# A retention layer and a multiplicative feed-forward block on one core: key copies moved between engines, and one chunk's outputs put inside an output block

## The chip, the cores and the metric

The kernel runs on one core of a Trainium2 chip. The metric is the device time of one execution in microseconds (us); of several executions the median is taken. A core has TensorE (PE, matrix products, with its weight loads shown as PEld), VectorE (DVE), ScalarE (ACT) and GpSimd (POOL), and SyncE (SP), which here issues the transfers. Matrix products land in PSUM, which is divided into banks; GpSimd works on SBUF only in this kernel.

## What is computed

The reference has two parts. The first is a recurrence over 768 positions for 4 batches and 8 heads of 64 elements: a state decays by a head's own factor and takes in the outer product of key and value, and the query reads it. The second part takes the 3072 resulting rows of 512 through a feed-forward block whose hidden layer is the product of two projections.

```python
gamma = 1.0 - 2.0 ** (-5.0 - np.arange(H, dtype=np.float32))
for t in range(S):
    state = gamma[None, :, None, None] * state + np.einsum('bhd,bhe->bhde', k[:, :, t], v[:, :, t])
    y[:, :, t] = scale * np.einsum('bhd,bhde->bhe', q[:, :, t], state)
# ... y becomes x, 3072 rows of 512
a = x @ w1
b = x @ w2
h = a * b @ w3
return h @ w_out
```

## The kernel before

The recurrence is worked in chunks of 128 positions, 6 to a batch, 24 in all. For a chunk n the kernel casts keys to f16 (`k16`), transposes them on TensorE into a padded form `KP` in which the two heads of a pair lie in separate halves, forms the scores of keys against queries and masks them (`am`), scales the values (`VP`), and forms the outputs from `am`, `VP` and the state. The feed-forward work is cut into units, "a", "b" and "o" (512 columns of output for 128 rows). They wait in a queue, and each chunk's step pulls some of them between its own parts, so that TensorE has work while other engines prepare. Since `w3 @ w_out` has no nonlinearity before it, it is multiplied once at the start (`W3O`).

The first four chunks are loaded two to a tile (a pair), with even and odd positions interleaved. Each half of a chunk's keys therefore either stays on its 64 partitions or is moved to the other 64 ("moved"):

```python
def pair_casts(n, moved, names="kv", eng=None):
    m, c = divmod(n, 2)
    rows = slice(c * 64, c * 64 + 64)
    t = 1 - c if moved else c
    to = slice(t * 64, t * 64 + 64)
    eng = eng or (nc.vector if moved else nc.gpsimd)
    # ... k16s[n] is allotted
    if "k" in names:
        eng.tensor_copy(
            k16s[n][to, :].rearrange("i (h d) -> i h d", d=D),
            pair_in["k", m][rows, :].rearrange("i (h t d) -> i h t d", t=2, d=D)[:, :, t, :],
        )
    for r in range(2 if "v" in names else 0):
        eng.tensor_tensor(VP[n % 3][to, :, r, r * 64 : r * 64 + 64], ...)   # cut: values times decay

def transposes_back(n):
    kp, ps = KP[n % 2], kTs.pop(n)
    nc.scalar.copy(kp[0:64, :, 0, :], ps[0:64, :, :])
    cast_to(kp[64:128, :, 1, :], ps[64:128, :, :], False)     # False: ScalarE, True: VectorE
```

The part of the start in which chunks 2 and 3 are prepared, in program order. Each engine does its own share of it in this order:

```python
for n in (2, 3):
    pair_casts(n, False, "k")            # GpSimd
    pair_casts(n, True, "k")             # VectorE
by_rows(W1, ps, 2)                       # TensorE, first projection of block 0
q_back = q_transposes(1, True)
q_back(0)                                # VectorE: qT
q_back(1)
by_rows(W1, ps, 3, blocks=(0, 3))
transposes(2)                            # TensorE, then the two copies of transposes_back
by_rows(W1, ps, 3, blocks=(3, 8))
transposes_front(3, "psK")
# ...
nc.gpsimd.tensor_copy(W2[0][:, :], w2_st[0][:, :])
pair_casts(2, False, "v")                # GpSimd
pair_casts(3, False, "v")
cast_to(pa[0], ps[0], False)
cast_to(pa[1], ps[1], True)              # VectorE
cast_to(pa[2], ps[2], False)
scores(2, between=lambda: pair_casts(2, True, "v"))   # VectorE: am, two vp, am
cast_to(pa[3], ps[3], True)
transposes_back(3)
# ... casts of W2
by_rows(W2, ps, 0)
outputs(2, "psK")
scores(3)
```

The step of a later chunk, and an output unit:

```python
def step(n):
    # ...
    scores(n)
    fill.pull(share * 0.25, ready)
    t_new = kv(n)
    # ... casts, transfers of later chunks
    if n == 4:
        transposes(5)
    fill.pull(share * 0.25, ready)
    outputs(n)
    Tst[0] = t_new
    if n != 4:
        transposes(n + 1)
    fill.pull(share * 0.5, ready)

def o_unit(self, tb, between=None):
    psO = ps_f.tile([128, DM], FP, tag="psF", name="psO")
    for f in range(8):
        if f == 4 and between:
            between()
        nc.tensor.matmul(psO[:, :], lhsT=self.HT[:, f, tb * 128 : (tb + 1) * 128], rhs=W3O[f][:, :],
                         start=(f == 0), stop=(f == 7))
    # ... scaled copy by ScalarE and the transfer out
```

The last output unit is made in two column blocks, `for c0, c1 in ((0, 320), (320, 512))`.

Of the kernel before, what the change touches and what calls it, by code (L numbers as in the profile page):

```python
# [18 lines left out]
def kernel(  # L19
# [11 lines left out]
    nc = tc.nc  # L31
# [194 lines left out]
    def cast_to(dst, src, on_dve):  # L226
        if on_dve:
            nc.vector.tensor_copy(dst, src)
        else:
            nc.scalar.copy(dst, src)  # L230
# [11 lines left out]
    def bank(tag, shape, dtype, name):  # L242
        return (ps_t if tag == "psT" else ps_at).tile(shape, dtype, tag=tag, name=name)
# [59 lines left out]
# [7 lines that stand above are left out]
        if n not in k16s:  # L310
            k16s[n] = att.tile([128, 512], HP, tag="k16", name="k16", bufs=3)
        if "k" in names:
            eng.tensor_copy(
                k16s[n][to, :].rearrange("i (h d) -> i h d", d=D),
                pair_in["k", m][rows, :].rearrange("i (h t d) -> i h t d", t=2, d=D)[:, :, t, :],
            )
        for r in range(2 if "v" in names else 0):
            eng.tensor_tensor(  # L318
                VP[n % 3][to, :, r, r * 64 : r * 64 + 64],
                pair_in["v", m][rows, :].rearrange("j (p s t e) -> j p s t e", s=2, t=2, e=64)[:, :, r, t, :],  # L320
                VS2[rows, t, :].rearrange("j (p s) -> j p s", s=2)[:, :, r].unsqueeze(2).broadcast_to((64, NP, 64)),
                MULT,
            )
# [9 lines left out]
    def casts(n):  # L333
        if n >= NSTEP:
            return
        k32, v32 = chunk_in.pop(n)
        if n % 2 == 0:
            q_cast(n // 2)
        k16 = att.tile([128, 512], HP, tag="k16", name="k16", bufs=3)
        nc.gpsimd.tensor_copy(k16[:, :], k32[:, :])  # L340
        vp = VP[n % 3]

        for r in range(2):
            nc.gpsimd.tensor_tensor(  # L344
                vp[:, :, r, r * 64 : r * 64 + 64],
                v32[:, :].rearrange("j (p s e) -> j p s e", s=2, e=64)[:, :, r, :],
                VS[:, :].rearrange("j (p s) -> j p s", s=2)[:, :, r].unsqueeze(2).broadcast_to((128, NP, 64)),
                MULT,
            )
        k16s[n] = k16  # L350
# [30 lines left out]
    def by_dma(n):  # L381

        return n >= DT0 and n != DT0 + 1
# [16 lines left out]
    def queries(n, p):  # L400
        if n < DT0:
            return qTs[n][:, p, :]
        c = n % 2
        return qTd[n // 2][:, :, p, c * 64 : (c + 1) * 64]

    def transposes(n, tag="psT"):
        if n >= NSTEP:
            return
        if by_dma(n):
            kT, kp = kTs.pop(n), KP[n % 2]  # L410
            nc.scalar.copy(kp[0:64, :, 0, :], kT[0:64, :, :])  # L411
            nc.scalar.copy(kp[64:128, :, 1, :], kT[64:128, :, :])
            return
        transposes_front(n, tag)
        transposes_back(n)

    def transposes_front(n, tag):
        k16 = k16s[n]
        ps = bank(tag, [128, NP, 128], HP, "psT")
        for p in range(NP):  # L420
            nc.tensor.transpose(ps[:, p, :], k16[:, p * 128 : (p + 1) * 128], ident16[:, :])
        kTs[n] = ps

    def transposes_back(n):
        kp, ps = KP[n % 2], kTs.pop(n)
        nc.scalar.copy(kp[0:64, :, 0, :], ps[0:64, :, :])
        cast_to(kp[64:128, :, 1, :], ps[64:128, :, :], False)

    def scores(n, tags=("psA0", "psA1"), between=None):
        kp = KP[n % 2]  # L430
        am = att.tile([128, NP, 2, 128], HP, tag="am", name="am")
        for half in range(2):
            ps = bank(tags[half], [128, 2, 2, 128], FP, "psA")
            for i in range(2):
                p = half * 2 + i
                for r in range(2):
                    nc.tensor.matmul(  # L437
                        ps[:, i, r, :], lhsT=kp[:, p, r, :], rhs=queries(n, p), start=True, stop=True
                    )
            if half and between:  # L440
                between()
            nc.vector.tensor_tensor(  # L442
                am[:, half * 2 : half * 2 + 2, :, :].rearrange("j p s i -> j (p s) i"),
                ps[:, :, :, :].rearrange("j p s i -> j (p s) i"),
                (keep2 if n < 4 else keep)[:, :].unsqueeze(1).broadcast_to((128, 4, 128)),
                MULT,
            )
        ATs[n] = am

    def kv(n, tag="psK", eng=nc.gpsimd):  # L450
        k16, vp = k16s.pop(n), VP[n % 3]
        c = n % NCH
        if c == NCH - 1:
            return None
        ps = bank(tag, [128, NP, 128], FP, "psK")
        for p in range(NP):

            rhs = vp[:, p, :, :].rearrange("j s e -> j (s e)")
            rhs = bass.AP(rhs.tensor, rhs.offset, [list(rhs.ap[0]), [192, 2], [1, 64]])
            nc.tensor.matmul(  # L460
                ps[:, p, :], lhsT=k16[:, p * 128 : (p + 1) * 128], rhs=rhs, start=True, stop=True
            )
        t16 = att.tile([128, NP, 128], HP, tag="t16", name="t16")
        if c == 0:
            nc.vector.tensor_tensor(t16[:, :, :], ps[:, :, :], GS[:, :, :], MULT)
        else:
            s32 = att.tile([128, NP, 128], FP, tag="s32", name="s32")
            nc.vector.tensor_tensor(s32[:, :, :], ps[:, :, :], Tst[0][:, :, :], ADD)  # L468
            eng.tensor_tensor(t16[:, :, :], s32[:, :, :], GS[:, :, :], MULT)  # L469
        return t16  # L470

    def outputs(n, tag="psY"):
        am, vp = ATs.pop(n), VP[n % 3]
        c = n % NCH
        ps = bank(tag, [128, NP, 128], FP, "psY")
        for p in range(NP):
            nc.tensor.matmul(ps[:, p, :], lhsT=vp[:, p, 0, :], rhs=am[:, p, 0, :], start=True, stop=False)  # L477
            nc.tensor.matmul(ps[:, p, :], lhsT=vp[:, p, 1, :], rhs=am[:, p, 1, :], start=False, stop=(c == 0))  # L478
            if c > 0:
                nc.tensor.matmul(ps[:, p, :], lhsT=Tst[0][:, p, :], rhs=queries(n, p), start=False, stop=True)  # L480
        if n % 2 == 0:
            XT[n // 2] = xpool.tile([128, NP, 256], HP, tag="xt", name="xt")

        order = "p a (t i) -> p a t i"
        nc.vector.tensor_tensor(  # L485
            XT[n // 2][:, :, n % 2 * C : (n % 2 + 1) * C].rearrange("p a (i t) -> p a t i", t=2),
            ps[:, :, :].rearrange(order, t=2), YS[:, :, :].rearrange(order, t=2), MULT,
        )
# [107 lines left out]
    fill = Queue()  # L596
# [3 lines left out]
    def step(n):  # L600

        ready = n * C
        share = fill.available(ready) / (2 - n % 2)
        if n >= DT0 - 2:
            casts(n + 2)
# [3 lines that stand above are left out]
        if n < DT0 - 2:  # L609
            casts(n + 2)  # L610
        dma_transposes(n + 2)
        load_chunk(n + 4)
        if n % 2:
            q_transposes((n + 1) // 2)
        if n == 4:
            transposes(5)
        fill.pull(share * 0.25, ready)
        outputs(n)
        Tst[0] = t_new
        if n != 4:  # L620
            transposes(n + 1)
        fill.pull(share * 0.5, ready)

# [44 lines left out]
    cast_w3(7, w3_st[7])  # L668
    q_cast(0)
    pair_casts(0, False, "k")  # L670
    pair_casts(1, False, "k")
    pair_casts(0, False, "v")
# [28 lines left out]
    ffn = [Ffn(a, b - a) for a, b in zip(bounds, bounds[1:])]  # L701
# [5 lines left out]
    def four_banks(tags):  # L707
        got = []
        for t in tags:
            if t == "psF":  # L710
                got.append(ps_f.tile([128, 2, TB], FP, tag=t, name="psF"))
            else:
                got.append(bank(t, [128, 2, TB], FP, "psG"))
        return [t[:, :, :] for t in got]
# [10 lines left out]
    ps = four_banks(("psF", "psF", "psF", "psY"))  # L725
# [2 lines left out]
    by_rows(W1, ps, 1)  # L728
    for n in (2, 3):
        pair_casts(n, False, "k")  # L730
        pair_casts(n, True, "k")
    by_rows(W1, ps, 2)
    q_back = q_transposes(1, True)
    q_back(0)
# [18 lines left out]
    ps = four_banks(("psF", "psF", "psF", "psT"))  # L753
# [73 lines left out]
```

## Time and profile before

| | before |
|---|---|
| time, median of 3 | 196.28 us (195.66 to 196.31) |
| span of the profiled execution | 193.8 us |
| TensorE busy | 185.0 us (95%) |
| VectorE busy | 118.6 us (61%) |
| ScalarE busy | 98.8 us (51%) |
| GpSimd busy | 86.1 us (44%) |
| granted TensorE clock | 1.000 |

The lines of the profile name an engine, a line of the kernel, an operation, what it writes and reads (out<-in, by tile names), and shapes as partitions x elements and type; in square brackets stands the idle time of that engine just ahead, and what ended it. xN is the number of instructions merged into a row. Busy time of TensorE counts a matmul up to its modelled end, so consecutive ones overlap: how fast they follow each other is read from their starts. A wait that is put down to one engine may have been for another, when several had to be over.

### The profile page before, as it was taken

Reading aid. Unit: us, or ns where it says so; the run is one execution under the profiler, and the core shown is the slowest. Engines: PE = TensorE matmul, PEld = TensorE weight load, DVE = VectorE, ACT = ScalarE, POOL = GpSimd, SP = SyncE. Lnnn points to the kernel's source line nnn. Section 1 sums busy time; section 2 is a strip of 40 time slices with the busy share of each in tenths; the row PEclk is TensorE's granted clock in tenths of the full one; section 3 lists DMA queues with packets and bytes.
Section 4 is the critical chain, followed back from the end, with each engine's and each line's share of the span. In section 5 each row is a group of like instructions: output and inputs, shape, how many; then the busy total and the mean of one; then the engine's idle time right before and its main releaser. Section 6 shows DMA issues by size and latency. Waiting matters only on the chain.

```text
span 193.8 us, 4696 instructions
## 1 busy us (share of the span) xinstructions
PE 185.0 (95%) x1777; PEld 140.0 (72%) x1777; DVE 118.6 (61%) x221; ACT 98.8 (51%) x191; POOL 86.1 (44%) x146
## 2 busy tenths in 40 slices
PE   6798999879999999999999999999999999999993
PEld 2435658668796889778877787788778877887752
DVE  3226598799586768657565666575657665754220
ACT  6478565582454455355535554555455545533322
POOL 7600287828863738368152643852426432200000
PEclk9999999999999999999999999999999999999999
DMA  5999999999999999999999989969979931111004
GB/s 203 370 391 390 300 395 324 365 286 223 219 172 226 214 230 240 98 274 223 215 268 206 209 187 225 212 148 244 212 186 195 209 95 26 57 54 54 36 28 156
DMA packets 85030, 40.54 MB, mean 209 GB/s; under 512 B 61328, under 2 KB 80016, under 8 KB 85008
## 3 DMA queue, kind: packets, MB, share of 16 engines
q1 hardware_dynamic: 85008, 40.25, 89.5%
q8 instruction: 14, 0.23, 0.5%
q14 instruction: 8, 0.07, 0.2%
HBM read 29.36 MB, written 6.29 MB: 184 GB/s over the span
## 4 chain that ended last, share of the span: by engine, by line
PE 79%; DMA 10%; SPq 4%; ACT 2%; DVE 2%; POOL 1%; issue 1%; ACTq 0%; POOLq 0%
PE psF L508 39%; PE psO L534 20%; DMA stg<-in_moe_w_dram 5%; PE psA L437 5%; DMA q<-in_q_dram 4%; SPq L62 4%; PE psY L477 3%; PE psY L478 2%; PE psY L480 2%; PE psK L460 2%; DVE am L442 1%; PE psF L719 1%; PE psW L293 1%; PE psG L508 1%; PE psO L551 1%
## 5 line engine op out<-in xcount | busy, mean ns | idle before, releaser
L508 PE MATMUL psF<-xt,w 128*128 128x256 f16 (+1 forms) x736 | 85.0, 266 | 0.0
L508 PEld LDWEIGHTS <-w 128*128 128x128 f16 x768 | 68.2, 98 | 7.2
L524 DVE TENSOR_TENSOR ht<-pa,psF 128x256 f16<-128x256 f32 x88 | 36.5, 416 | 22.1 <-PE psF L508 12.9
L518 ACT COPY pa<-psF 128x256 f32<-128x256 f32 x84 | 31.2, 372 | 33.8 <-PE psF L508 33.4
L442 DVE TENSOR_TENSOR am<-psA,keep 128x512 f16<-128x512 f32 x48 | 31.0, 685 | 23.0 <-PE psA L437 22.8
L534 PE MATMUL psO<-w3o,ht 128*128 128x512 f16 x184 | 43.1, 379 | 0.0
L469 POOL TENSOR_TENSOR t<-s,GS 128x512 f16<-128x512 f32 x15 | 19.3, 1284 | 40.0 <-DVE s L468 40.0
L539 ACT ACTIVATE osb<-psO 128x512 f32<-128x512 f32 x23 | 13.7, 597 | 37.8 <-PE psO L534 37.8
L534 PEld LDWEIGHTS <-ht 128*128 128x128 f16 x184 | 17.9, 98 | 17.2 <-DVE ht L768 0.2
L344 POOL TENSOR_TENSOR vp<-v,VS 128x256 f16<-128x256 f32 x40 | 23.8, 616 | 5.5 <-DMA v<-in_v_dram 2.5
L327 POOL CAST q<-q 128x1024 f16<-128x1024 f32 x12 | 13.0, 1086 | 27.5 <-DMA q<-in_q_dram 27.5
L485 DVE TENSOR_TENSOR xt<-psY,YS 128x512 f16<-128x512 f32 x24 | 17.8, 742 | 3.6 <-PE psY L480 3.2
L477 PE MATMUL psY<-am,vp 128*128 128x128 f16 x96 | 16.8, 219 | 0.9 <-ACT kp L230 0.5
L478 PE MATMUL psY<-am,vp 128*128 128x128 f16 x96 | 16.7, 219 | 0.4 <-DVE vp L318 0.4
L437 PEld LDWEIGHTS <-kp 128*128 128x128 f16 x192 | 12.5, 98 | 5.3 <-ACT kp L230 0.9
L340 POOL CAST k<-k 128x512 f16<-128x512 f32 x20 | 12.2, 612 | 5.0 <-PE psK L460 3.4
L468 DVE TENSOR_TENSOR s<-psK,t 128x512 f32<-128x512 f32 x16 | 11.0, 688 | 3.0 <-PE psK L460 2.7
L251 DVE COPY w3t<-psW 128x1024 f16<-128x1024 f16 x8 | 5.5, 690 | 10.7 <-PE psW L259 8.4
L437 PE MATMUL psA<-qTd,kp 128*128 128x128 f16 x144 | 11.1, 219 | 0.0
L480 PE MATMUL psY<-qTd,t 128*128 128x128 f16 x60 | 10.8, 219 | 0.0
L411 ACT COPY kp<-kT 64x512 f16<-64x512 f16 x17 | 10.5, 618 | 0.4
L478 PEld LDWEIGHTS <-vp 128*128 128x128 f16 x96 | 9.4, 98 | 1.8 <-POOL vp L318 0.7
(80 smaller groups left out, 192.8 us busy)
## 6 DMA issues: line engine op xcount, KB each, us to landing
stg<-in_moe_w_dram SPq DMA_DIRECT2D x16, 512.0 KB, 7.8
q<-in_q_dram SPq DMA_DIRECT2D x12, 512.0 KB, 5.6
out_dram<-osb SPq DMA_DIRECT2D x23, 256.0 KB, 2.9
k<-in_k_dram SPq DMA_DIRECT2D x20, 256.0 KB, 5.4
v<-in_v_dram SPq DMA_DIRECT2D x20, 256.0 KB, 5.4
stg<-in_moe_w_out_dram SPq DMA_DIRECT2D x4, 512.0 KB, 8.0
stg<-in_k_dram SPq DMA_DIRECT2D x2, 512.0 KB, 10.5
stg<-in_v_dram SPq DMA_DIRECT2D x2, 512.0 KB, 8.0
```

Of the source, the lines that this page charges most:

```text
L344: nc.gpsimd.tensor_tensor(vp[:, :, r, r * 64 : r * 64 + 64], v32[:, :].rearrange("j (p s e) -> j p s e", s=2, e=64)[:, :, r, :], VS[:, :]. ...
L437: nc.tensor.matmul(ps[:, i, r, :], lhsT=kp[:, p, r, :], rhs=queries(n, p), start=True, stop=True)
L442: nc.vector.tensor_tensor(am[:, half * 2 : half * 2 + 2, :, :].rearrange("j p s i -> j (p s) i"), ps[:, :, :, :].rearrange("j p s i -> j ( ...
L469: eng.tensor_tensor(t16[:, :, :], s32[:, :, :], GS[:, :, :], MULT)
L477: nc.tensor.matmul(ps[:, p, :], lhsT=vp[:, p, 0, :], rhs=am[:, p, 0, :], start=True, stop=False)
L478: nc.tensor.matmul(ps[:, p, :], lhsT=vp[:, p, 1, :], rhs=am[:, p, 1, :], start=False, stop=(c == 0))
L480: nc.tensor.matmul(ps[:, p, :], lhsT=Tst[0][:, p, :], rhs=queries(n, p), start=False, stop=True)
L485: nc.vector.tensor_tensor(XT[n // 2][:, :, n % 2 * C : (n % 2 + 1) * C].rearrange("p a (i t) -> p a t i", t=2), ps[:, :, :].rearrange(orde ...
L508: nc.tensor.matmul(ps[:, i * w : (i + 1) * w], lhsT=W[d][:, (f + i) * 128 : (f + i + 1) * 128], rhs=XT[self.tok0 // TB][:, d, c0 : c0 + w] ...
L518: nc.scalar.copy(self.pa[f][:, :], ps[:, :])
L524: nc.vector.tensor_tensor(self.HT[:, f : f + TB // self.width, :].rearrange("p f n -> p (f n)"), self.pa.pop(f)[:, :], ps[:, :], MULT,)
L534: nc.tensor.matmul(psO[:, :], lhsT=self.HT[:, f, tb * 128 : (tb + 1) * 128], rhs=W3O[f][:, :], start=(f == 0), stop=(f == 7),)
```

## The change

The change has three parts in the program. The moved key casts of chunks 2 and 3 go from VectorE to ScalarE, to relieve VectorE at that point. The copy of the second half of chunk 2's padded keys goes from ScalarE to VectorE, so that the two halves are on two engines. In the step of chunk 5, the next queued output unit is taken out of the queue, and the chunk's outputs (with the padded-key copies of chunk 6) are issued between its fourth and fifth matmul; before, the outputs came first and the unit after. The amount of work is the same. The words that come with the change also speak of the last block as 320 + 192 columns; that is in the kernel before already, and the diff has no line for it.

```diff
@@ -310,7 +310,7 @@
         if "k" in names:
-            eng.tensor_copy(
+            (nc.scalar.copy if eng is nc.scalar else eng.tensor_copy)(
                 k16s[n][to, :].rearrange("i (h d) -> i h d", d=D),
                 pair_in["k", m][rows, :].rearrange("i (h t d) -> i h t d", t=2, d=D)[:, :, t, :],
             )
@@ -424,7 +424,7 @@
     def transposes_back(n):
         kp, ps = KP[n % 2], kTs.pop(n)
         nc.scalar.copy(kp[0:64, :, 0, :], ps[0:64, :, :])
-        cast_to(kp[64:128, :, 1, :], ps[64:128, :, :], False)
+        cast_to(kp[64:128, :, 1, :], ps[64:128, :, :], n == 2)
@@ -615,9 +615,14 @@
         fill.pull(share * 0.25, ready)
-        outputs(n)
+        if n == 5:
+
+            fill.units.pop(0)
+            ffn[1].o_unit(0, lambda: [outputs(n), transposes(6)])
+        else:
+            outputs(n)
         Tst[0] = t_new
-        if n != 4:
+        if n not in (4, 5):
             transposes(n + 1)
         fill.pull(share * 0.5, ready)
@@ -728,7 +733,7 @@
     for n in (2, 3):
         pair_casts(n, False, "k")
-        pair_casts(n, True, "k")
+        pair_casts(n, True, "k", nc.scalar)
```

## The prediction

> **What bounds the kernel now.** I read the page first, then the busy time by stretch, then the waits of TensorE alone, and last the timeline of the two places where TensorE waits. From the page:
>
> ```profile
> PE   6798999879999999999999999999999999999993
> PE 79%; DMA 10%; SPq 4%; ACT 2%; DVE 2%; POOL 1%; issue 1%; ACTq 0%; POOLq 0%
> ```
>
> The first line is TensorE's busy share in 40 slices of 4.85 us; after the eighth it is full to the last one. The second is the chain of work that ended last: 79% of it is TensorE. So time can be won only where TensorE waits. The busy time by stretch says where that is (columns: stretch and its length, then busy us of TensorE, weight loads, VectorE, ScalarE, GpSimd):
>
> ```profile
> 33.00:42.00 9.00, 7.33 (x81) 5.62 (x79) 7.18 (x13) 5.74 (x9) 6.46 (x8) 1.00 1.09 349
> 42.00:57.00 15.00, 15.00 (x206) 12.77 (x204) 12.00 (x23) 6.69 (x14) 10.64 (x14) 1.00 1.05 214
> 57.00:62.00 5.00, 4.79 (x60) 3.59 (x58) 3.44 (x7) 1.98 (x4) 2.33 (x4) 1.00 0.88 197
> 62.00:180.00 118.00, 118.00 (x1147) 94.92 (x1145) 74.97 (x144) 58.92 (x127) 51.53 (x68) 1.00 0.92 178
> ```
>
> From 33 to 42 us TensorE lacks 1.67 us, from 57 to 62 us 0.21 us, and from 62 to 180 us nothing. The change touches just the first and the third stretch. In the first, TensorE's own waits are:
>
> ```profile
> PE psY L477 <- ACT kp L230: 0.5, 1, 0.5
> PE psY L478 <- DVE vp L318: 0.4, 1, 0.4
> PE psA L437 <- ACT kp L230: 0.4, 1, 0.4
> PE psY L477 <- DVE am L442: 0.2, 1, 0.2
> ```
>
> They all belong to chunk 2. Its timeline (start, duration, engine, line, out<-in):
>
> ```profile
> 34.45 1.17 DVE L313 CAST k<-stg 64x512 f16<-64x512 f32 x2 [1.10 <-DMA stg<-in_k_dram]
> 34.48 1.62 POOL L313 CAST k<-stg 64x512 f16<-64x512 f32 x2 [0.24 <-DMA stg<-in_k_dram]
> 35.39 0.40 PE L421 MATMUL psT<-ident,k 128*128 128x128 f16 x4
> ...
> 35.54 0.74 DVE L228 COPY qT<-psTq 128x512 f16<-128x512 f16 x2
> ...
> 35.88 0.58 ACT L426 COPY kp<-psT 64x512 f16<-64x512 f16 x1 [3.70 <-PE psT L421]
> ...
> 36.20 0.67 DVE L228 COPY stg<-psF 128x512 f32<-128x512 f32 x1
> 36.48 0.58 ACT L230 COPY kp<-psT 64x512 f16<-64x512 f16 x1
> ...
> 37.50 0.69 DVE L442 TENSOR_TENSOR am<-psA,keep 128x512 f16<-128x512 f32 x1 [0.62 <-PE psA L437]
> 37.52 2.70 POOL L318 TENSOR_TENSOR vp<-stg,VS 64x256 f16<-64x256 f32 x4 [0.33 <-PE psA L437]
> ...
> 38.22 1.52 DVE L318 TENSOR_TENSOR vp<-stg,VS 64x256 f16<-64x256 f32 x2
> ```
>
> The reader should follow one string through these lines: keys land, k is cast, PE transposes it, ScalarE copies one half of kp (35.88) and only then the other (36.48, done 37.06), scores, am, and then VectorE scales the values (vp), which ends at 39.74. The second am ends at 40.46, and the last outputs of chunk 2 start at 40.52. The first wait in the list above, put down to kp, is really one for VectorE's vp: kp was done at 37.06, the first of the two vp at about 38.98. In the other stretch:
>
> ```profile
> 58.00 1.29 DVE L442 TENSOR_TENSOR am<-psA,keep 128x512 f16<-128x512 f32 x2
> 58.03 0.61 PE L508 MATMUL psF<-xt,w 128*128 128x128 f16 x8
> ...
> 58.75 0.22 PE L477 MATMUL psY<-am,vp 128*128 128x128 f16 x1
> ...
> 59.35 0.22 PE L477 MATMUL psY<-am,vp 128*128 128x128 f16 x1
> ...
> 59.68 1.89 PE L534 MATMUL psO<-w3o,ht 128*128 128x512 f16 x8
> ```
>
> Chunk 5's outputs stand right behind its scores and one b unit. They start only when the first am is done, and their second half only when the second am is (58.00 + 1.29 = 59.29). No wait view lists this, because the tail of the matmul before covers the gap; it shows in the start times.
>
> **What the Trainium skill says.** (1) "TensorE: Matmul & The Clock Gate", section "Back-to-back issue gap": an isolated warm matmul takes N/2.4 + 2.5 ns, 56 ns for 128 columns and 216 ns for 512. The trace agrees: starts are 0.055 us apart at 128 columns (58.75, 58.80, 58.86), and the eight 512-column ones take 59.68 to 61.40, 0.215 each. I use these steps below. (2) "GPSIMD Engine Reference", section "1. Specifications": GpSimd shares its SBUF interfaces with VectorE and suffers when VectorE runs in a two-port mode. The trace agrees: VectorE's key cast of this form took 420 ns before GpSimd had begun and 719 ns beside it; GpSimd's own took from 607 ns (the shortest of four) to 860 ns. (3) "VectorE: DVE Perf Modes", section "Why PSUM operands drop a tier": from PSUM VectorE keeps at most the packed 2x mode, so an f16 copy stays quick there. The trace: 406 to 408 ns for a 128x512 f16 copy of q from PSUM, against 578 to 580 ns for ScalarE's copies of the same length. (4) "PSUM — Partial Sum Buffer", section "PSUM bank collisions raise a hardware error": two engines may use one bank at once only in different groups of 32 partitions. The halves of kp are partitions 0 to 63 and 64 to 127, so the hardware lets both copies run at once; but no engine pair in the trace before reads one bank together, so it does not show whether this program's generated waits let them.
>
> **The change, part by part.**
>
> *Moved casts to ScalarE.* Removed from VectorE: two casts, 1.17 us from 34.45. Added to ScalarE, idle for 3.70 us until 35.88: two copies of 512 elements; its copies of that length take 0.58, so 34.45 to 35.03 and to 35.62 (an estimate; no f32 SBUF copy of that size is in the trace). GpSimd, now alone, should need about 0.61 each: 34.48 to 35.09 to 35.70 instead of 36.10. Chunk 2's transposes can start at about 35.17 instead of 35.39, behind the three matmuls before them. psT is ready at about 35.60 and ScalarE's half of kp runs 35.66 to 36.24, 0.22 earlier. VectorE can copy qT from about 34.97 (psTq was complete near 34.92), to 35.78.
>
> *Second half of kp to VectorE.* If both run together: 35.78 to 36.19 at 0.41 each, beside ScalarE's. Scores then have both halves at 36.24 and start at 36.28 instead of waiting to 37.12. VectorE casts pa from 36.19 to 36.86 and does the first am at about 36.87 to 37.56, 0.63 earlier than 37.50 to 38.19. Earlier than this hardly helps: the values of chunks 2 and 3 were issued at 30.83 us and took 6.6 us in the view of DMA issues, so vp cannot start before 37.43 (GpSimd's did at 37.52). vp: 37.58 to 39.10; second am to 39.82; last outputs 0.64 earlier. I allow 0.6 to 0.7 us.
>
> From there on TensorE runs without a gap and VectorE too, up to 48 us, and both start earlier by the same amount. What could stop the shift is a landing. The view of DMA issues gives 43.03 + 5.3 = 48.3 for chunk 5's values (used by GpSimd at 51.0) and 46.91 + 5.8 = 52.7 for chunk 6's (used at 53.7). The latter leaves 1.0 us, enough for 0.65. The last w2 tile is cast by 42.57 and used at 44.16. I let the shift pass whole.
>
> *Outputs of chunk 5 inside an output block.* No instruction is added. Four 512-column matmuls (4 x 0.216 = 0.86 us) now stand between the b unit and the outputs. Without waits the outputs would have started at 58.03 + 8 x 0.055 = 58.47 and ended at 58.47 + 12 x 0.055 = 59.13; the block began at 59.68, so 0.55 us is lost now. After: block's first half 58.47 to 59.33; outputs from 59.33, second half from 59.66, after am's 59.29. Both waits vanish: 0.55 us. xt would be ready about 60.9 and is used after chunk 6's scores at 61.3. It fits.
>
> *320 + 192.* The last block is cut that way already in the kernel before; the diff does not touch it. Zero.
>
> Sum with the copies together: 0.65 + 0.55 = 1.2 us, 196.28 - 1.2 = 195.1 us.
>
> **The rivals.** *The two kp copies are put in order* (one PSUM bank, two engines, ScalarE's first). Then VectorE waits to 36.26, copies to 36.67, casts pa to 37.34, and the first am runs 37.36 to 38.05: only 0.14 earlier, as VectorE itself is what am waits for. With 0.55 that is 0.7 us, 195.6. For it: a bank is the unit that a cautious generator would guard; against it: the halves lie on different partitions. I give it 45%. *The values' transfer takes the place of the wait*: vp starts at 37.43 at the earliest, so part one can't yield more than 38.22 - 37.43 = 0.8 us. This caps the gain at 1.35 us, 194.9. *ScalarE becomes the bound*: its casts reach to 35.62, psT is ready at 35.60, so it costs some 0.05 us; if a cast took the 1.05 us of the page's 1024-element casts, kp would be 0.8 us later, chunk 2 would lose about 0.6 us and the total would be 196.3. The 0.585 us of a 512-element f32 copy from PSUM speaks against it (10%). *The shift is swallowed by later loads*: GpSimd waits for q, k and v from 62.24 on, but chunk 8's casts end near 66 and its scores come several us later; nothing in TensorE's row shows it (10%).
>
> **Range and chances.** Weighing 195.1 (half), 195.6 (most of the rest) and the small chances of no gain gives 195.3; I take 195.2. The runs of before spread from 195.66 to 196.31, so the time itself is uncertain by some 0.3. Range 194.5 to 195.9. A change of 2% is 3.9 us, more than all of TensorE's idle time in both stretches (1.67 + 0.21), so faster by that is 0.01, slower 0.02, within 0.97.
>
> **What would show it.** Right: VectorE's kp copy near 36 us overlapping ScalarE's; scores at about 36.3; last outputs of chunk 2 near 39.9; four 512-column matmuls ahead of chunk 5's outputs and no uneven start times in them; TensorE full in 57 to 62. Wrong: kp on VectorE after 36.25 (the ordered rival); vp still at 38.1 or later; a TensorE wait after 42 us; a ScalarE cast much longer than 0.6 us; or a new TensorE gap around the output block.

## The result, and the profile after

| | before | changed |
|---|---|---|
| time, median | 196.21 us (195.66 to 196.31, 4 runs) | 195.09 us (195.02 to 195.39, 4 runs) |
| ratio to before | | 0.9952, 95% interval 0.993 to 0.9973 |
| span of the profiled execution | 193.8 us | 193.0 us |
| start of chunk 2's key casts (the landing of its keys) | 34.45 us | 34.44 us |
| from there to the last two output pairs of chunk 2 | 6.07 us | 5.58 us |
| from chunk 5's scores to the unit behind chunk 6's scores | 4.27 us | 4.00 us |
| from the key casts to the end of the span | 159.36 us | 158.59 us |

The changed kernel is 0.5% faster. By the interval that is 0.53 to 1.37 us (0.27% and 0.70% of 196.21). The last four rows are read from start times in the timelines; the end of the span is taken from the trace in full (193.81 and 193.04 us), while the recorded expectations go by the page's figure, rounded to 0.1. The rows are counted from the key casts because the keys' landing differs from execution to execution (34.44 to 35.26 us in the profiles of this study), and everything behind it moves along.

First TensorE's busy share in 40 slices and the chain that ended last, from the page of the changed kernel:

```profile
PE   6789999789999999999999999999999999999993
PE 70%; DMA 17%; POOL 4%; DVE 3%; SPq 2%; issue 1%; ACT 1%; POOLq 0%; DVEq 0%; ACTq 0%
```

TensorE is full as before, but its share of the chain fell from 79% to 70% and transfers rose from 10% to 17%: just before 60 us the chain now reaches back from TensorE, through ScalarE's copies, into the transposing transfer of chunk 6's keys and the load of its values. The busy time by stretch (same columns as before):

```profile
33.00:42.00 9.00, 7.18 (x84) 5.79 (x82) 6.37 (x12) 6.40 (x10) 5.72 (x8) 1.00 1.10 351
42.00:57.00 15.00, 15.00 (x209) 12.78 (x206) 12.00 (x22) 6.67 (x14) 11.29 (x14) 1.00 1.01 210
57.00:62.00 5.00, 4.91 (x58) 3.66 (x56) 3.72 (x8) 2.49 (x5) 1.83 (x4) 1.00 0.96 194
```

Between 33 and 42 us TensorE is busy for less than before (7.18 against 7.33 us), although it starts 84 matmuls there instead of 81. Busy time doesn't show the gain, starts do: the last two output pairs of chunk 2 began at 40.52 us before and begin at 40.02 now. TensorE's waits in that stretch, and chunk 2's timeline:

```profile
PE psY L478 <- DVE vp L318: 0.6, 1, 0.6
PE psT L421 <- POOL k L313: 0.4, 1, 0.4
PE psY L477 <- ACT kp L230: 0.4, 1, 0.4
PE psA L437 <- DVE kp L228: 0.2, 1, 0.2
PE psY L477 <- DVE am L442: 0.2, 1, 0.2
```

```profile
34.44 1.26 ACT L313 CAST k<-stg 64x512 f16<-64x512 f32 x2 [2.29 <-DMA stg<-in_k_dram]
34.48 1.28 POOL L313 CAST k<-stg 64x512 f16<-64x512 f32 x2 [0.72 <-PE psTq L366]
...
35.21 0.38 PE L421 MATMUL psT<-ident,k 128*128 128x128 f16 x4 [0.43 <-POOL k L313]
...
35.68 0.58 ACT L426 COPY kp<-psT 64x512 f16<-64x512 f16 x1
...
36.29 0.43 DVE L228 COPY kp<-psT 64x512 f16<-64x512 f16 x1 [1.05 <-ACT kp L426]
...
36.75 0.69 DVE L228 COPY stg<-psF 128x512 f32<-128x512 f32 x1
...
37.36 0.68 DVE L442 TENSOR_TENSOR am<-psA,keep 128x512 f16<-128x512 f32 x1
37.52 2.78 POOL L318 TENSOR_TENSOR vp<-stg,VS 64x256 f16<-64x256 f32 x4 [0.62 <-DVE stg L228]
...
38.07 1.17 DVE L318 TENSOR_TENSOR vp<-stg,VS 64x256 f16<-64x256 f32 x2
```

Three things are to be seen. VectorE's copy of kp begins at 36.29, just as ScalarE's ends (35.68 + 0.58 = 36.26), after an idle time of 1.05 us that ScalarE's copy ended: the two copies run in order. Behind it VectorE casts pa and does am, which thus starts only 0.14 us earlier than before (37.50). And the scaling of the values (vp) takes 1.17 us instead of 1.52, though it is the same pair of instructions beside the same GpSimd work: that 0.35 us is the larger part of the 0.49 us that chunk 2 gains.

At chunks 5 and 6, the timeline has:

```profile
57.50 1.29 DVE L442 TENSOR_TENSOR am<-psA,keep 128x512 f16<-128x512 f32 x2
...
57.97 1.03 PE L534 MATMUL psO<-w3o,ht 128*128 128x512 f16 x4
...
59.37 0.62 ACT L411 COPY kp<-kT 64x512 f16<-64x512 f16 x1 [1.72 <-DMA kT<-k]
59.50 1.03 PE L534 MATMUL psO<-w3o,ht 128*128 128x512 f16 x4
...
60.01 0.61 ACT L412 COPY kp<-kT 64x512 f16<-64x512 f16 x1
60.37 0.88 PE L437 MATMUL psA<-qTd,kp 128*128 128x128 f16 x8
```

Half of the output block stands ahead of chunk 5's outputs now, and half behind. But chunk 6's eight score matmuls, 0.61 us before (61.40), take 0.88 us: the second half of kp is ready only at 60.62, because ScalarE waited 1.72 us for the transposed keys of chunk 6. So 0.27 us of the gain was given back in this execution. The keys were issued late and landed slowly: their transfer was issued at 54.13 us and took 5.2 us, so they landed near 59.3.

### The profile page after: what moved, and what is told of

Read it like the earlier page. It is cut to its first block, busy times and chain, and to the rows that moved or that the text cites. A ratio compares the mean times of both kernels' runs of the same rounds, so it can differ in the third digit from the quotient of the medians.

```text
span 193.0 us, 4697 instructions
## 1 busy us (share of the span) xinstructions
PE 184.5 (96%) x1777; PEld 139.6 (72%) x1777; DVE 117.4 (61%) x220; ACT 99.5 (52%) x192; POOL 85.6 (44%) x146
## 4 chain that ended last, share of the span: by engine, by line
PE 70%; DMA 17%; POOL 4%; DVE 3%; SPq 2%; issue 1%; ACT 1%; POOLq 0%; DVEq 0%; ACTq 0%
PE psF L508 36%; PE psO L534 18%; DMA stg<-in_v_dram 5%; DMA stg<-in_moe_w_dram 5%; PE psA L437 4%; DMA v<-in_v_dram 4%; DMA kT<-k 3%; SPq L62 2%; PE psY L477 2%; PE psY L478 2%; POOL vp L318 2%; PE psY L480 2%; PE psK L460 2%; PE psF L724 1%; DVE am L442 1%
## 5 line engine op out<-in xcount | busy, mean ns | idle before, releaser
L411 ACT COPY kp<-kT 64x512 f16<-64x512 f16 x17 | 10.5, 618 | 2.5 <-DMA kT<-k 2.1
L412 ACT COPY kp<-kT 64x512 f16<-64x512 f16 x17 | 10.5, 615 | 0.4
```

## Theory, rivals and experiments

Theory: (a) the copies of kp run in order because both read one PSUM bank, so moving one to VectorE brings nothing, and the casts' move brings all of chunk 2's gain; (b) the output block brings its 0.53 us whatever is done for chunk 2; (c) the wait of chunk 6's scores comes from a load that happened to land late. Rivals: the copy on VectorE is what helps; the block's gain is taken back by chunk 6's keys; the change itself delays that load.

Each experiment is a variant of the changed kernel. "Chunk 2" is the time from the key casts to the last two output pairs, "chunks 5, 6" from chunk 5's scores to the unit behind chunk 6's, "to the end" from the key casts to the end of the span, and "v6" how long the issue of chunk 6's values took, all from one profiled execution of each, in us:

| run | chunk 2 | chunks 5, 6 | to the end | v6 | median us | ratio to before (95%) |
|---|---|---|---|---|---|---|
| before | 6.07 | 4.27 | 159.36 | 1.33 | 196.21 | |
| changed | 5.58 | 4.00 | 158.59 | 3.30 | 195.09 | 0.9952 (0.993 to 0.9973) |
| e1_casts | 5.52 | 4.27 | 158.79 | 2.33 | 195.5 | 0.9966 (0.9953 to 0.9979) |
| e2_casts_half | 5.57 | 4.27 | 158.84 | 3.80 | 195.59 | 0.9971 (0.9958 to 0.9984) |
| e3_block | 6.07 | 3.74 | 158.80 | 1.73 | 195.58 | 0.9966 (0.995 to 0.9982) |
| e4_no_half | 5.52 | 3.80 | 158.45 | 3.59 | 194.93 | 0.9941 (0.9924 to 0.9958) |
| e5_two_banks | 5.48 | 3.74 | 158.24 | 1.43 | 194.92 | 0.9934 (0.9914 to 0.9955) |
| e6_split6 | 5.57 | 4.14 | 158.73 | 3.31 | 195.8 | 0.9978 (0.9966 to 0.999) |
| e7_banks_split6 | 5.47 | 4.14 | 158.62 | 2.08 | 195.71 | 0.9985 (0.9968 to 1.0002) |
| e9_no_half_split6 | 5.53 | 4.15 | 158.70 | 1.78 | 195.35 | 0.996 (0.995 to 0.997) |
| e10_kp6_first | 5.53 | 3.74 | 158.27 | 1.93 | 194.98 | 0.9955 (0.9938 to 0.9972) |
| e11_banks_delay | 5.49 | 3.74 | 158.25 | 1.42 | 195.12 | 0.9954 (0.9942 to 0.9965) |
| e12_banks_kp6_first | 5.49 | 3.73 | 158.24 | 1.34 | 194.69 | 0.9932 (0.9919 to 0.9944) |
| e13_changed_again | 5.58 | 3.74 | 158.33 | 1.94 | 195.15 | 0.9961 (0.995 to 0.9972) |

The kernel before ran beside each group: median 196.22 us beside e1 to e4, 196.34 beside e5 to e9, 196.0 beside e10 to e13. The ratios overlap for many pairs; where one tenth of a us decides, I go by the profile's stretches. That of chunk 2 repeats to 0.02 us among kernels that treat chunk 2 alike; that of chunks 5 and 6 doesn't (4.00 and 3.74 us in two executions of the changed kernel).

### The parts one by one

**e1_casts**: only the key casts move.

```diff
-        cast_to(kp[64:128, :, 1, :], ps[64:128, :, :], n == 2)
+        cast_to(kp[64:128, :, 1, :], ps[64:128, :, :], False)
# and chunk 5's step as before: outputs(n), then transposes(n + 1) and the queue
```

> Only the key casts go to ScalarE; both kp copies of chunk 2 stay on ScalarE and chunk 5's outputs stay ahead of the output block. Theory (the two kp copies are put in order because they read one PSUM bank, so the move of the second copy gains next to nothing, and behind it VectorE casts pa late): the second kp is done near 36.86 us, the scores wait for it to about 36.9, VectorE casts pa already near 36.1, the first am starts near 37.3 and the last outputs of chunk 2 start at 40.0 +- 0.15, as in the changed kernel (40.02); time 0.4 to 0.6 us below before. Rival (the copy on VectorE is what brings the gain): last outputs at 40.3 or later, time within 0.25 us of before.

Keys landed 0.6 us later here, so the absolute times stand 0.6 us later too; the stretch counts. Part of the timeline of this run:

```profile
36.49 0.69 DVE L228 COPY stg<-psF 128x512 f32<-128x512 f32 x1 [0.64 <-POOL k L313]
36.88 0.58 ACT L230 COPY kp<-psT 64x512 f16<-64x512 f16 x1
...
37.90 0.69 DVE L442 TENSOR_TENSOR am<-psA,keep 128x512 f16<-128x512 f32 x1 [0.72 <-PE psA L437]
38.11 2.74 POOL L318 TENSOR_TENSOR vp<-stg,VS 64x256 f16<-64x256 f32 x4 [0.54 <-PE psA L437]
...
38.62 1.17 DVE L318 TENSOR_TENSOR vp<-stg,VS 64x256 f16<-64x256 f32 x2
```

VectorE casts pa (36.49) while ScalarE still copies, and am starts 37.90 - 35.04 = 2.86 us after the key casts, against 2.92 in the changed kernel and 37.50 - 34.45 = 3.05 before. The casts alone bring 6.07 - 5.52 = 0.55 us, a little more than with the copy moved. The theory holds; the rival's 40.3 would have been a stretch of 5.85 or more. The time fell by 0.72 us, more than the 0.4 to 0.6 expected.

**e2_casts_half**: casts and copy, without the block.

```diff
-        if n == 5:
-            fill.units.pop(0)
-            ffn[1].o_unit(0, lambda: [outputs(n), transposes(6)])
-        else:
-            outputs(n)
+        outputs(n)
```

> Key casts on ScalarE and the second kp copy on VectorE; chunk 5's outputs stay ahead of the output block. Theory: last outputs of chunk 2 start near 40.02 us, the waits of chunk 5's outputs for am remain (0.55 us lost), the scores of chunk 6 do not wait for kp since they come 0.5 us later; time 0.5 us below before. Rival (the padded keys of chunk 6 are late by chance, whatever comes before): the scores of chunk 6 wait here too, and time is 0.3 us below before.

Chunk 2 took 5.57 us, as in the changed kernel: against e1 the copy costs 0.05 us and wins nothing. The time is 0.63 us below before (0.5 expected). Chunk 6's keys were late here as well, kp was done at 60.14 + 0.61 = 60.75, but the scores came at 61.16 and didn't wait. So the lateness is there without the block; only the earlier scores run into it.

**e3_block**: only the block, casts and copy as before.

> Only chunk 5's outputs inside the output block; chunk 2 as before. Theory: the last outputs of chunk 2 stay at 40.5 us, the uneven starts in chunk 5's outputs go away (0.55 us), scores of chunk 6 start near 60.85 and wait for the padded keys by less than 0.1 us; time 0.45 to 0.55 us below before. Rival (what the block wins, the padded keys of chunk 6 take back): scores of chunk 6 end as late as before less 0.2 us, time within 0.25 us of before.

Chunk 2 stays at 6.07, chunks 5 and 6 take 3.74 instead of 4.27: the block brings 0.53 us and there is no wait behind it. Time is 0.64 us below before (195.58 against 196.22; 0.45 to 0.55 expected).

**e4_no_half**: casts and block, the copy stays on ScalarE.

> The change without the move of the second kp copy to VectorE. Theory: as fast as the changed kernel within 0.15 us (1.0 to 1.2 us below before), the last outputs of chunk 2 at 40.0 +- 0.15 us. Rival (the copy on VectorE brings part of the gain): 0.3 us or more slower than the changed kernel.

Its median is 1.29 us below that of before; chunk 2 is 5.52, and the scores of chunk 6 wait a little (3.80). These two stretches gain 1.02 us together, of which 0.91 is left at the end; another 0.10 is lost ahead of chunk 8's scores, and why stays open. The kernel is at least not slower than the changed kernel: no sign of a gain from the copy.

### Why the copy brings nothing

**e5_two_banks**: the keys of chunk 2 are transposed twice, so that each copy reads a bank of its own.

```diff
-    transposes(2)
+    transposes_front(2, "psT")
+    first_bank = kTs[2]
+    transposes_front(2, "psA0")
+    second_bank, kTs[2] = kTs[2], first_bank
+    transposes_back(2, second_bank)       # VectorE's half reads second_bank
```

> The changed kernel, with chunk 2's keys transposed twice, into two PSUM banks, so that ScalarE and VectorE each copy their half of kp from a bank of their own (four transposes more, 0.22 us of TensorE). From the start of chunk 2's key casts to the start of the last two pairs of its outputs took 6.07 us before and 5.58 in the changed kernel. Theory (one bank keeps the copies in order): VectorE's copy starts within 0.3 us of ScalarE's and overlaps it, VectorE casts pa and does the first am about 0.35 us earlier, and that stretch is 5.1 to 5.3 us. Rival (VectorE waits for something else, or the values' landing holds the scaling anyway): VectorE's copy still starts after ScalarE's ended, or the stretch stays at 5.5 or more.

```profile
35.98 0.58 ACT L426 COPY kp<-psT 64x512 f16<-64x512 f16 x1
36.22 0.43 DVE L228 COPY kp<-psT 64x512 f16<-64x512 f16 x1 [0.68 <-PE psF L724]
...
37.29 0.68 DVE L442 TENSOR_TENSOR am<-psA,keep 128x512 f16<-128x512 f32 x1
...
37.81 2.70 POOL L318 TENSOR_TENSOR vp<-stg,VS 64x256 f16<-64x256 f32 x4 [0.60 <-DMA stg<-in_v_dram]
38.00 1.46 DVE L318 TENSOR_TENSOR vp<-stg,VS 64x256 f16<-64x256 f32 x2
```

The copies overlap now (36.22 is before 36.56), so reading one bank was what put them in order. The order is the program's own: in the trace of the changed kernel VectorE's copy waits for one count only, which ScalarE alone raises, and in the four kernels with this copy and one bank (changed, e2, e6, e13) it begins 0.03 us after ScalarE's ends. The second bank is also a second tile, so this run doesn't tell whether the waits go by the bank or by the tile. The first am starts 2.54 us after the key casts (37.29 - 34.75) instead of 2.92, 0.38 earlier (about 0.35 expected). Yet the stretch fell by 0.10 only, to 5.48: the size of the expectation failed. The scaling took 1.46 us instead of 1.17. It was not late: it began at 38.00, right behind am (37.29 + 0.68 = 37.97), while the values had landed by 37.81, when GpSimd began its own scaling. What it gained at its start it lost beside GpSimd's instruction, as the next run shows. So both are true: the shared bank orders the copies, and undoing that brings little, because GpSimd's scaling begins with the values' landing and VectorE's has to fit in with it. (Against before, the stretch is 0.59 us shorter: with the copies really together, the prediction's 0.6 to 0.7 us is about what comes out.)

**e11_banks_delay**: the same, with an idle memset of 192 elements on VectorE ahead of the scaling.

```diff
-    scores(2, between=lambda: pair_casts(2, True, "v"))
+    scores(2, between=lambda: [nc.vector.memset(spare[:, :], 0.0), pair_casts(2, True, "v")])
```

> Two banks for chunk 2's transposed keys, and an idle VectorE memset of 192 elements (a tile that nothing reads, some 0.2 to 0.3 us) between the first am and the scaling of chunk 2's values. Theory (how long VectorE's scaling takes depends on where in GpSimd's instruction of the same kind it begins: 0.50 to 0.56 us after GpSimd's start the first of the two took 0.42 us, at 0.19 it took 0.70 and at 0.70 it took 0.76): starting 0.45 to 0.55 us after GpSimd's, the two take 1.17 us instead of 1.46, so the delay costs less than 0.1 us and the stretch from the key casts to chunk 2's last outputs stays at 5.4 to 5.55. Rival (its length goes with something else, such as ScalarE's copies beside it): it stays at 1.46 and the stretch is 5.7 or more.

The memset took 0.22 us, the scaling began 0.39 us after GpSimd's (not the 0.45 to 0.55 aimed at), and took 1.25. The stretch is 5.49 against 5.48: a delay of 0.20 us of the scaling costs 0.01. The first of the two instructions shows why (starts and ends in us after the start of GpSimd's first instruction, which ends at 0.61; its second begins at 0.57 and, in the kernels of the last row, ends at 1.18):

| runs | start | took | end |
|---|---|---|---|
| e5_two_banks | 0.19 | 0.704 | 0.89 |
| e11_banks_delay | 0.39 | 0.499 | 0.89 |
| e4_no_half | 0.50 | 0.420 | 0.92 |
| changed | 0.55 | 0.419 | 0.97 |
| before, e3_block | 0.70 | 0.762, 0.761 | 1.46 |

All rows fit one rule: it ends 0.42 us after its own start, or 0.28 us after the end of the GpSimd instruction under way, whichever is later (0.61 + 0.28 = 0.89; 1.18 + 0.28 = 1.46). In the changed kernel it begins at 0.55, just ahead of GpSimd's second instruction, and goes first; before, it began at 0.70, behind it, and waited. VectorE's second instruction of the pair always meets a GpSimd instruction, and in all 14 profiles it ends 0.28 us after that one. GpSimd waits in the same way: its second instruction ends 0.47 us after VectorE's first where that went first (0.97 and 1.45 in the changed kernel). So for this pair of operations the two engines take turns, a whole instruction each. The sharing as such is in the Trainium skill, "GPSIMD Engine Reference", section "1. Specifications" (the two engines share their SBUF interfaces), and these numbers agree with it. That the turns are whole instructions is read from these traces; e11 is the only run that moved one start on purpose.

### The wait of chunk 6's scores

**e6_split6**: VectorE copies the second half of chunk 6's padded keys.

```diff
             nc.scalar.copy(kp[0:64, :, 0, :], kT[0:64, :, :])
-            nc.scalar.copy(kp[64:128, :, 1, :], kT[64:128, :, :])
+            cast_to(kp[64:128, :, 1, :], kT[64:128, :, :], n == 6)
```

> The changed kernel, with the second half of chunk 6's padded keys copied by VectorE instead of ScalarE (they come from SBUF, where no bank orders the two). Theory (the scores of chunk 6 now wait for the second kp copy, whose keys' transposing transfer is issued late because the SyncE queue is held up by an earlier load): the wait in chunk 6's scores is gone, from the first matmul of chunk 5's scores to the end of chunk 6's takes 3.74 us instead of 4.0, and the span is 0.2 to 0.3 us shorter counted from the key casts (158.3 instead of 158.56). Rival (the wait is hidden again later): span from the key casts unchanged within 0.1.

This failed, by an error of mine that the timeline shows at once:

```profile
59.92 0.74 DVE L485 TENSOR_TENSOR xt<-psY,YS 128x512 f16<-128x512 f32 x1 [0.59 <-PE psY L480]
60.59 0.22 PE L437 MATMUL psA<-qTd,kp 128*128 128x128 f16 x1
60.69 0.29 DVE L228 COPY kp<-kT 64x512 f16<-64x512 f16 x1
```

In program order the copy stands behind xt on VectorE, and xt waits for chunk 5's outputs. The copy, 0.29 us long, starts at 60.69, after the scores began. The wait is now fixed in place instead of depending on a load.

**e7_banks_split6** adds e6's edit to e5_two_banks, and **e9_no_half_split6** adds it to e4_no_half.

> Both additions to the changed kernel: two banks for chunk 2's transposed keys, VectorE for half of chunk 6's padded keys. Theory: gains add, 0.35 + 0.27: from the key casts to the end of the span 157.9 to 158.1 us (159.35 before, 158.56 changed), time near 194.5. Rival (the earlier TensorE gets, the more the loads of chunks 6 and 7 hold it up): 158.4 or more, and a wait for kp or vp between 55 and 75 us.

> Chunk 2's second kp copy stays on ScalarE, with key casts and output block as in the change, and VectorE copies half of chunk 6's padded keys. Theory: sum of the single gains, 0.55 for the casts and 0.53 for the block without the wait of chunk 6: from key casts to the end 158.2 to 158.3 us, time near 194.9. Rival (the casts' gain is taken back by the loads): 158.5 or more.

Both missed for the same reason: chunks 5 and 6 take 4.14 and 4.15 us, 0.4 more than without a wait, although the keys landed in time in both. The numbers of e7's rival came true (158.62 us to the end), but not its cause: the issue of chunk 6's values was short (2.08).

**e10_kp6_first**: e4_no_half with that half on VectorE, issued ahead of the outputs.

```diff
-            ffn[1].o_unit(0, lambda: [outputs(n), transposes(6)])
+            ffn[1].o_unit(0, lambda: [transposes(6), outputs(n)])
```

> Second kp copy of chunk 2 on ScalarE; VectorE's half of chunk 6's padded keys is now issued ahead of chunk 5's outputs, so that it does not stand behind xt, which waits for those outputs. Theory (in the two runs with the half behind xt it started 0.1 us after the scores, at xt's end, whether the transfer was late or not): the half is done within 0.35 us of the landing of kT, the scores of chunk 6 don't wait, from key casts to the end 158.2 to 158.35 us, time at or under that of the casts with the block (194.9). Rival (VectorE has no room there: it delays am or xt): 158.5 us or more, with a new wait of TensorE after 57 us.

```profile
59.43 0.29 DVE L228 COPY kp<-kT 64x512 f16<-64x512 f16 x1
59.79 1.03 PE L534 MATMUL psO<-w3o,ht 128*128 128x512 f16 x4
59.99 0.74 DVE L485 TENSOR_TENSOR xt<-psY,YS 128x512 f16<-128x512 f32 x1 [0.26 <-PE psY L480]
60.65 0.61 PE L437 MATMUL psA<-qTd,kp 128*128 128x128 f16 x8
```

The order was the cause: the copy stands ahead of xt, which still starts at once behind the outputs, and the scores take 0.61 again. One part of the expectation failed: the copy ended at 59.72, 1.5 us after the keys were there (ScalarE's half began at 58.22), not within 0.35, because VectorE had chunk 5's am and a feed-forward product to do first. The keys landed in time here, so this run doesn't show what the move is worth when they are late.

**e12_banks_kp6_first**: e5_two_banks with that edit.

> Two banks for chunk 2's transposed keys and VectorE's half of chunk 6's padded keys ahead of chunk 5's outputs. Theory: chunk 2's stretch 5.48 us as with two banks alone, no wait in chunk 6's scores, from key casts to the end 158.15 to 158.3 us, time 194.7 to 195.0, the best of all. Rival (nothing is left to win there): within 0.1 us of the two banks alone, 194.9 to 195.1.

It has the lowest median, 194.69 us, ratio 0.9932 (0.9919 to 0.9944); the changed kernel beside it in the same group had 0.9961 (0.995 to 0.9972). But e5_two_banks, in another group, has the same ratio, 0.9934, and the same 158.24 us to the end, so the rival stands: that the copy of chunk 6's keys wins anything over two banks alone is not shown. The profiles of e12 and of the changed kernel beside it differ by 0.09 us (158.24 and 158.33), all of it in chunk 2, as neither had late keys. Whether other executions of e12 avoid such a wait is not shown.

**e13_changed_again**: the changed kernel once more.

> The changed kernel once more, beside the three others. Theory (the late landing of chunk 6's values is chance: in ten profiles the issue of that load took 1.3 to 3.8 us, with the same program ahead of it in several): chunk 2's stretch is 5.58 us again and the wait in chunk 6's scores differs from 0.27, by the issue of that load; time 195.0 to 195.3. Rival (the change itself delays that load): its issue takes over 3 us again and the wait is 0.2 to 0.3 us again.

```profile
58.02 0.62 ACT L411 COPY kp<-kT 64x512 f16<-64x512 f16 x1
...
58.66 0.62 ACT L412 COPY kp<-kT 64x512 f16<-64x512 f16 x1
...
60.84 0.61 PE L437 MATMUL psA<-qTd,kp 128*128 128x128 f16 x8
```

Chunk 2 repeats to 5.58, but kp is done at 59.28, long before the scores, and these take 0.61 us. The issue of chunk 6's values took 1.94 us instead of 3.30. Where it took over 3 us (changed, e2, e4, e6), the transposing transfer of chunk 6's keys was issued 19.56 to 20.02 us after the key casts, against 18.71 to 19.32 in the other profiles. The issue isn't all: in the changed profile that transfer also took 5.2 us to land, against 4.0 here. The same program has the issue long and short, and so does e9_no_half_split6 (1.78) against e4_no_half (3.59), which are one program up to chunk 6's padded keys. So the 0.27 us is no fixed price of the change. That the change doesn't make it more frequent is not shown: the issue took over 3 us in 4 of the 12 profiles with the key casts on ScalarE and in neither of the two without (before, e3). Why it is sometimes held up stays open.

## Why the prediction was right, and where not

- **Predicted 195.2 us, range 194.5 to 195.9; measured 195.09.** The size was right partly by luck: one step failed and one term was wrong in the other direction, and for chunk 2 the two nearly cancel (0.49 us instead of 0.6 to 0.7).
- **"The second half of kp to VectorE", worked out with both copies running together, failed.** It was put at 0.6 to 0.7 us. The copies ran in order, as the first rival said (given 45%), and its times came out to the hundredth: the copy after 36.26, am at 37.36. e5 shows that reading from one bank (and one tile) is the reason. The Trainium skill, "PSUM — Partial Sum Buffer", section "PSUM bank collisions raise a hardware error", says that two engines may use one bank at once in different groups of 32 partitions; no run here shows them doing so, as the program's own waits put the copies in order.
- **The rival's own size was too small.** It gave 0.14 us for chunk 2; measured 6.07 - 5.58 = 0.49. The term that was mis-sized is the scaling of the values, taken as 1.52 us: it took 1.17. 0.14 + 0.35 = 0.49. Starting 0.15 us earlier relative to GpSimd (0.55 instead of 0.70) put it ahead of GpSimd's second instruction.
- **The turns could be seen in the trace before.** The prediction says that VectorE's key cast took 420 ns "before GpSimd had begun"; GpSimd had begun at 34.48, 0.03 us behind it. VectorE's first cast went through (to 34.87), GpSimd's took 0.86 us (to 35.34), and VectorE's second, 719 ns, ended at 35.62, 0.28 us after that: the same 0.28 as in the scaling.
- **One wait was misread, without effect.** The first wait of chunk 2's list was taken for one for VectorE's vp (38.98), as kp was done at 37.06. That is chunk 2's kp; the wait ended with ScalarE's copy of chunk 3's (38.66 + 0.58 = 39.24; the matmul starts at 39.29). The matmul behind it waits for VectorE's vp all the same, to 39.89.
- **The moved casts** took 0.617 us each on ScalarE (predicted 0.58), from 34.44 to 35.70 (35.62); GpSimd's ended at 35.76 (35.70), transposes began at 35.21 (35.17), ScalarE's kp at 35.68 (35.66). They carry the whole of chunk 2's gain, 0.55 us alone in e1, by way of the scaling: it begins 0.51 us behind GpSimd's there, instead of 0.70.
- **The output block**, 0.55 us predicted, brings 0.53 (e3_block and e13_changed_again against before). Right.
- **"I let the shift pass whole"** holds for TensorE between 42 and 57 us. The margin that I worked out for chunk 6's values (landing 52.7, used at 53.7) was that of one execution: in the changed profile they landed at 46.32 + 7.6 = 53.9, and GpSimd waited for them, without loss to TensorE. The late landing that did cost time, that of chunk 6's keys, was not among those that the prediction checked.
- **The last block as 320 + 192**: nothing, as the diff says.
- **Sum**: 0.49 + 0.53 = 1.02 us, and from before to e13 the whole way to the end is 159.36 - 158.33 = 1.03 shorter. In the first profile 0.27 is lost again, 0.75 by the sum and 159.36 - 158.59 = 0.77 measured. The times' interval, 0.53 to 1.37, holds all of these.

## What to carry to other kernels

Two engines that copy two halves out of one PSUM bank may be put in order by the program's own waits, and the second then stands in the way of its engine's next work; look for an idle time of the second that the first one ended before counting on an overlap. A copy that is to catch a wait has to stand ahead of whatever waits longer in its engine's order (e6 against e10). And where TensorE waits for a chain of small steps, putting independent matmuls ahead of the wait is the safe gain: it brought 0.53 us in each kernel that had it and whose next keys were copied in time.

## What was not expected of the hardware

The same pair of VectorE instructions took 1.17, 1.25, 1.46 or 1.52 us depending on where in GpSimd's instructions they began, to 0.01 us in repetition (1.17 or 1.18 in the eight profiles that began 0.50 to 0.56 us behind). Beginning later by 0.20 us, in e11, cost the chunk 0.01 us; beginning 0.15 us later than in the changed kernel, as before the change, makes the first instruction end 0.49 us later. A small shift of one engine can thus pay more, or less, than itself.
